# Gate and value products by Strassen's seven products over pairs of 512-token groups, in two runs, with the converted weights kept in scratch memory

## The chip, the cores and the metric

The kernel runs on one core of a Trainium2 chip. The metric is the device time of one execution in microseconds (us). The engines are TensorE (PE in the rows: matmuls; PEld: its weight loads, which run beside the matmuls), VectorE (DVE), ScalarE (ACT), GpSimd (POOL), and SyncE (SP), which issues nearly all transfers.

## The reference: what is computed

An attention-like stage without a softmax makes `x`, 2304 tokens by 512 features. Two layers follow:

```python
h = x @ w_in                                   # 512 -> 2048
g = np.where(h > 0.0, h, np.exp(np.minimum(h, 0.0)) - 1.0)
x = g @ w_out                                  # 2048 -> 512
gate = 1.0 / (1.0 + np.exp(-(x @ w_gate)))     # 512 -> 1536
val = x @ w_val                                # 512 -> 1536
out = gate * val @ w_out2                      # 1536 -> 512
```

The weights come in as 64-bit floats; the kernel makes 32-bit ones of them on the chip. The change is in the second layer, the last four lines.

## The kernel before

**Numbers in two parts.** Each 32-bit operand is split into a high part (the value in TensorE's fp32r format) and a low part (the value minus that). `split` (L79) makes both: ScalarE writes the high part (L81), GpSimd or VectorE the low part (L82). `mm3` (L84) makes one product of three matmuls: high by high, high by low, low by high (L86, L87, L88).

**Tokens and features.** The 2304 tokens are four groups of 512 and one of 256. A layer's hidden features are taken in blocks `f` of 128: 16 in the first layer, 12 in the second. A pass takes two blocks and goes over all groups; the partial outputs of a pass are collected in PSUM tiles `acc` and then added to `y` in SBUF.

**Second layer.** For each block and group, `FF.ups` (L297) makes the gate product into a bank `h` and the value product into a bank `tv`: four blocks of input features by three matmuls each, so 24 matmuls. ScalarE takes the sigmoid of `h` (L314), VectorE multiplies by `tv` (L317), and the result is split into a tile `g` (L81, L82). Two steps later `FF.downs` (L335) uses `g`: for each 128 tokens of the group one `mm3` against `w_out2`, 12 matmuls. In the second block of a pass `evac_b` (L365) copies the sums to `y` (L372) or adds them (L374), and in the last pass stores the rows (L377).

**Weights.** Each block of each weight matrix is loaded once as 512 KB of 64-bit words into one of two buffers `raw` (L111), and converted by `Weight.chain` (L113): two ScalarE instructions (L120, L121), four on VectorE (L123, L124, L127, L129), and a split. The steps of the chain are put between the instructions of the matmul steps. A raw buffer is free again after L129.

**What sets the order.** Everything is written out by hand. Each engine takes its instructions in the order of the program, so an instruction that waits holds up all that stand behind it on its engine. The transfers stand in SyncE's queue in the same way.

## Time and profile before

| | |
|---|---|
| median of 3 runs | 930.99 us (930.36 to 931.33) |
| span of the profiled execution, first to last instruction | 929.7 us |
| PE busy | 911.1 us, 98% |
| DVE, ACT, POOL busy | 469.3, 365.7 and 298.2 us |
| granted TensorE clock, mean | 0.998 |

The span is that of one execution that was profiled; the median of the runs is 1.3 us over it, for what lies before the first and behind the last instruction and from run to run. A busy share is an average over the span. In the rows below a time in us at the start of a row counts from the start of the span, and a matmul's duration includes its way through the array, which overlaps the next one: what one costs in a stream is the distance between two starts.

### The profile page before, as it was taken

To read this page: it belongs to the slowest core of one execution; us is meant where nothing else is said; L and a number is where in the kernel's file an instruction comes from. 1 tells how busy PE (TensorE), PEld (TensorE's weight loads), DVE (VectorE), ACT (ScalarE), POOL (GpSimd) and SP (SyncE) were. 2 spreads that over 40 slices of the span, in tenths; PEclk is the share of its full clock that TensorE was granted. 3 is DMA by queue.
4 is the path that set the end of the run, shared out by engine and by line. 5 is a ranking of instruction groups with operands and counts; after the bars stand their busy time and mean duration, and the time that the engine had idled before them with its cause. 6 is when DMAs were issued, how large, how long until landed. Compare 5 with 4: busy or idle time off the path is not lost.

```text
span 929.7 us, 15480 instructions
## 1 busy us (share of the span) xinstructions
PE 911.1 (98%) x6466; PEld 770.7 (83%) x6466; DVE 469.3 (50%) x759; ACT 365.7 (39%) x675; POOL 298.2 (32%) x259
## 2 busy tenths in 40 slices
PE   7899999999999999999999999999999999999998
PEld 5789988888888888888888888888888888888886
DVE  3767635555464555566884334444435354343223
ACT  2345565544545444545673333323223232221110
POOL 2245523332333333334563213222222233222111
PEclk9999999999999999999999999999999999999999
DMA  9655411210111111102121101111111012000113
GB/s 341 199 181 183 118 46 47 68 35 34 46 47 46 45 46 46 46 25 67 46 68 46 46 23 53 39 46 46 45 46 46 24 46 67 24 23 1 46 46 114
DMA packets 26999, 60.57 MB, mean 65 GB/s; under 512 B 6576, under 2 KB 7600, under 8 KB 26928
## 3 DMA queue, kind: packets, MB, share of 16 engines
q1 hardware_dynamic: 24864, 56.89, 19.0%
q10 hardware_dynamic: 2064, 2.67, 0.8%
q8 instruction: 51, 0.84, 0.4%
q14 instruction: 20, 0.16, 0.1%
HBM read 54.84 MB, written 4.72 MB: 64 GB/s over the span
## 4 chain that ended last, share of the span: by engine, by line
PE 93%; DVE 4%; ACT 1%; DMA 1%; POOL 0%; issue 0%; ACTq 0%; DVEq 0%; POOLq 0%
PE acc L86 12%; PE acc L87 12%; PE acc L88 12%; PE h L86 12%; PE h L88 12%; PE h L87 12%; PE tv L87 5%; PE tv L86 5%; PE tv L88 5%; PE to L194 3%; PE h L290 2%; DMA vt<-in_csmall 1%; PE ts L194 1%; DVE e L266 1%; DVE t L127 0%; DVE t L124 0%
## 5 line engine op out<-in xcount | busy, mean ns | idle before, releaser
L82 POOL TENSOR_TENSOR g<-e,g 128x512 fp32r<-128x512 f32 (+1 forms) x146 | 165.8, 1135 | 565.9 <-ACT g L81 526.3
L86 PE MATMUL h<-x,w 128*128 128x512 f32 (+1 forms) x520 | 192.5, 370 | 0.0
L88 PE MATMUL h<-x,w 128*128 128x512 f32 (+1 forms) x520 | 192.3, 370 | 0.0
L87 PE MATMUL h<-x,w 128*128 128x512 f32 (+1 forms) x520 | 192.3, 370 | 0.0
L81 ACT CAST g<-e 128x512 fp32r<-128x512 f32 (+1 forms) x148 | 82.5, 558 | 232.3 <-DVE e L317 154.7
L317 DVE TENSOR_TENSOR e<-e,tv 128x512 f32<-128x512 f32 (+1 forms) x60 | 38.1, 634 | 231.8 <-PE tv L88 231.8
L86 PE MATMUL acc<-g,w 128*128 128x512 f32 (+1 forms) x352 | 124.3, 353 | 1.2 <-ACT w L81 0.6
L88 PE MATMUL acc<-g,w 128*128 128x512 f32 (+1 forms) x352 | 124.0, 352 | 0.3 <-DVE w L82 0.2
L87 PE MATMUL acc<-g,w 128*128 128x512 f32 (+1 forms) x352 | 123.8, 352 | 0.0
L309 DVE SCALAR_TENSOR_TENSOR e<-e,h 128x512 f32<-128x512 f32 (+1 forms) x88 | 51.9, 590 | 134.8 <-ACT e L306 134.2
L87 PEld LDWEIGHTS h<-x,w 128*128 128x128 f32 x520 | 97.9, 188 | 17.7
L88 PEld LDWEIGHTS h<-x,w 128*128 128x128 f32 x520 | 98.0, 188 | 17.6
L86 PEld LDWEIGHTS h<-x,w 128*128 128x128 f32 x520 | 97.9, 188 | 17.6
L314 ACT ACTIVATE e<-h 128x512 f32<-128x512 f32 (+1 forms) x60 | 33.3, 555 | 154.5 <-PE h L88 150.7
L82 POOL TENSOR_TENSOR w<-t,w 128x512 fp32r<-128x512 f32 x65 | 86.6, 1332 | 8.9 <-ACT w L81 8.7
L305 ACT ACTIVATE e<-h 128x512 f32<-128x512 f32 (+1 forms) x88 | 45.8, 520 | 109.6 <-PE h L88 92.2
L87 PE MATMUL tv<-x,w 128*128 128x512 f32 (+1 forms) x240 | 88.7, 370 | 0.0
L86 PE MATMUL tv<-x,w 128*128 128x512 f32 (+1 forms) x240 | 88.6, 369 | 0.0
L88 PE MATMUL tv<-x,w 128*128 128x512 f32 (+1 forms) x240 | 88.6, 369 | 0.0
L87 PE MATMUL acc<-w,g 128*128 128x512 f32 x216 | 84.6, 392 | 0.0
L86 PE MATMUL acc<-w,g 128*128 128x512 f32 x216 | 84.6, 392 | 0.0
L88 PE MATMUL acc<-w,g 128*128 128x512 f32 x216 | 84.4, 391 | 0.0
(75 smaller groups left out, 1344.5 us busy)
## 6 DMA issues: line engine op xcount, KB each, us to landing
in<-in_ain SPq DMA_DIRECT2D x12, 1024.0 KB, 5.5
raw<-in_w_in SPq DMA_DIRECT2D x16, 512.0 KB, 3.5
raw<-in_w_out SPq DMA_DIRECT2D x14, 512.0 KB, 3.6
raw<-in_w_gate SPq DMA_DIRECT2D x12, 512.0 KB, 3.6
raw<-in_w_val SPq DMA_DIRECT2D x12, 512.0 KB, 3.5
raw<-in_w_o SPq DMA_DIRECT2D x12, 512.0 KB, 3.5
y<-in_ain SPq DMA_DIRECT2D x4, 1024.0 KB, 7.8
out<-y SPq DMA_DIRECT2D x8, 256.0 KB, 2.8
```

The lines of the kernel that those rows point to most:

```text
L81: act.copy(hi, src)
L82: lo_engine.tensor_tensor(out=lo, in0=src, in1=hi.bitcast(F32), op=ALU.subtract)
L86: pe.matmul(out_, wh, xh, start=start, stop=False, skip_group_check=shared)
L87: pe.matmul(out_, wh, xl, start=False, stop=False, skip_group_check=shared)
L88: pe.matmul(out_, wl, xh, start=False, stop=stop, skip_group_check=shared)
L194: return pe.matmul(out_, w, x, start=start, stop=True, skip_group_check=True)
L266: dve.tensor_tensor(out=self.xf.rearrange("d (p x i) -> d x p i", p=NP, x=2), in0=to[:, :, 256:].rearrange("d x (p i) -> d x p i", p=NP), ...
L290: pe.matmul(h, w[:, a, c[k]], x[:, b, k, t], start=i + k == 0, stop=i == 2 and k == KB - 1)
L305: act.activation(out=e, in_=h, func=AF.Relu, scale=-1.0)
L309: dve.scalar_tensor_tensor(out=e, in0=e, scalar=-1.0, in1=h, op0=ALU.add, op1=ALU.max)
L314: act.activation(out=e, in_=h, func=AF.Sigmoid)
L317: dve.tensor_tensor(out=e, in0=e, in1=v, op=ALU.mult)
```

## The change

**Seven products for eight.** Two groups of 512 tokens are a pair. The 512 input features are two halves, so the gate and value products of a pair and a block are a 2 by 2 by 2 product of blocks: eight block products, each of two feature blocks by three matmuls, 48 matmuls. Strassen's scheme (in Winograd's form) makes them of seven, 42 matmuls, from sums of the operands:

- four sums of the tokens' blocks (`Pair.sum`, names t1 to t4), once for each pair;
- four sums of the weights' blocks (`Sums.chain`, tile `s` with both its parts), once for each `f`;
- sums of the products. Three PSUM banks A, B and D are used in a `unit`; products 1, 6, 5 and 3 are accumulated in turn into A, which is copied to SBUF in between, and 7 and 4 into D.

The 256-token group keeps the plain products (`single`).

**Two runs.** The first run takes pair 0 (groups 0 and 1) and the last group through the twelve blocks, the second run takes pair 1 (groups 2 and 3). The weights are converted in the first run as before, and the converted tiles (`w` of gate, half of `w` of value, `s`, `w` of out2: 2.25 MB for each block) are stored to scratch memory (`save`). In the second run they are loaded again (`restore`). The operands of the pairs lie where the first layer's `x` was.

**Order.** The products against `w_out2` (`down`: 128 tokens, two blocks, six matmuls) are kept in a list and put between the products of the units two blocks later (`fill`). The steps of the weight chains of the next block are put between the products as well (`bg`). The split of a unit's results is issued in the next unit (`later`). The low part of the last group's results goes to a part of `x3`. The tiles `e`, `g`, `t` and `w` are taken from rings of named buffers; `e` has six.

```diff
-            t = tpool.tile([128, DM], I32, tag="t", name="t")
+            t = t_tile(self.at)
             f, u = t.bitcast(F32), t.bitcast(U32)
+            self.f = f
...
-            p = wpools[0] if self.i < 8 or (self.i - 8) % 12 >= 4 else wpools[1]
-            w = p.tile([128, 2, DM], F32R, tag="w", name="w")
+            w = w_tile(self.slot)
             split(w[:, 0, :], w[:, 1, :], f, lo_engine)
             self.w = w
...
+    class Sums:
+        def __init__(self, f):
+            self.f = f
+        def chain(self):
+            (g0, g1), (v0, v1) = ((t[:, : DM // 2], t[:, DM // 2 :]) for t in (W[n, self.f].f for n in "gv"))
+            dve.tensor_tensor(out=v1, in0=v0, in1=v1, op=ALU.add)
+            dve.tensor_tensor(out=v0, in0=g0, in1=v0, op=ALU.subtract)
+            yield
+            dve.tensor_tensor(out=g0, in0=v1, in1=g0, op=ALU.subtract)
+            dve.tensor_tensor(out=g1, in0=g1, in1=g0, op=ALU.subtract)
+            yield
+            w = s_tile(self.f)
+            split(w[:, 0, 0], w[:, 1, 0], W["v", self.f].f, pool)
+            split(w[:, 0, 1], w[:, 1, 1], W["g", self.f].f, pool)
+            self.w = w
+            yield
+    for f in range(FB):
+        W["g", f] = Weight(w_gate[f], f % 2 * 3, 0)
+        W["v", f] = Weight(w_val[f], f % 2 * 3 + 1, 1)
+        W["2", f] = Weight(w_o2[f], (2, 6, 5, 7)[f % 4], 2)
+        W["s", f] = Sums(f)
...
+        def sum(self, name):
+            a, b = {"t1": ("12", "11"), "t2": ("22", "t1"), "t3": ("22", "12"), "t4": ("21", "t2")}[name]
+            dve.tensor_tensor(out=self.f32(name), in0=self.f32(a), in1=self.f32(b), op=ALU.subtract)
+        def split(self, name, lo_engine):
+            p = self.place(name)
+            split(p[:, 0], p[:, 1], self.f32(name), lo_engine)
+            self.x[name] = p.rearrange("p i (k t) -> p i k t", k=KH)
+    UP = {1: ("11", "11"), 2: ("12", "21"), 3: ("s4", "22"), 4: ("22", "t4"), 5: ("s1", "t1"), 6: ("s2", "t2"), 7: ("s3", "t3")}
+    def product(i, pair, f, bank, start=False):
+        a, b = UP[i]
+        x = pair.x[b]
+        for k in range(KH):
+            if a[0] == "s":
+                t, at = {"s3": (0, 0), "s1": (0, 2), "s2": (1, 0), "s4": (1, 2)}[a]
+                w = W["s", f].w[:, :, t, (at + k) * 128 : (at + k) * 128 + 128]
+            else:
+                at = ((int(a[1]) - 1) * KH + k) * 128
+                w = W["gv"[int(a[0]) - 1], f].w[:, :, at : at + 128]
+            mm3(bank, w[:, 0], w[:, 1], x[:, 0, k], x[:, 1, k], start and k == 0, k == KH - 1, True)
...
+    def finish_later():
+        while later:
+            later.pop(0)()
+    def unit(pair, f, bg, fill):
+        A, B, D = u_bank(), u_bank(), u_bank()
+        s1, s2, s4, sg = (e_tile() for _ in range(4))
+        product(1, pair, f, A, True)
+        act.copy(s1, A)
+        finish_later()
+        fill(5)
+        bg()
+        product(2, pair, f, B, True)
+        dve.tensor_tensor(out=s1, in0=s1, in1=B, op=ALU.add)
+        bg()
+        fill(0)
+        product(7, pair, f, D, True)
+        bg()
+        product(6, pair, f, A)
+        act.copy(s2, A)
+        act.activation(out=s1, in_=s1, func=AF.Sigmoid)
+        bg()
+        fill(1)
+        product(5, pair, f, A)
+        act.copy(s4, A)
+        dve.tensor_tensor(out=s4, in0=s4, in1=D, op=ALU.add)
+        bg()
+        fill(2)
+        product(3, pair, f, A)
+        act.activation(out=sg, in_=A, func=AF.Sigmoid)
+        fill(3)
+        product(4, pair, f, D)
+        later.append(glu(pair.g + 1, f, sg, s4))
+        dve.tensor_tensor(out=s2, in0=s2, in1=D, op=ALU.add)
+        fill(4)
+        later.append(glu(pair.g, f, s1, s2))
+    def glu(g, f, a, b, engine=pool):
+        engine.tensor_tensor(out=a, in0=a, in1=b, op=ALU.mult)
+        def rest():
+            n = N[g]
+            if g == 4:
+                gt = x_of[3].rearrange("p i k t -> p (i k t)")[:, 2048 + f % 3 * 2 * n : 2048 + (f % 3 + 1) * 2 * n]
+                gt = gt.rearrange("p (i t) -> p i t", i=2)
+            else:
+                gt = g_tile()
+            gb[g, f] = gt
+            split(gt[:, 0], gt[:, 1], a, pool)
+        return rest
...
+    def down(fs, g, t, by):
+        a = acc_bank()
+        c = slice(t * 128, t * 128 + 128)
+        for f in fs:
+            x, w = gb[g, f], W["2", f].w
...
+        prep = {
+            a + 5: (("split", "11", dve), ("split", "21", pool)),
+            a + 7: (("sum", "t1"), ("sum", "t3"), ("split", "t1", dve), ("sum", "t2")),
+            a + 8: (("split", "t2", pool), ("split", "t3", dve)),
+            a + 9: (("split", "22", pool), ("sum", "t4")),
+        }
...
+        def background(f):
+            order = "gvgvgvgvgv2s2s2s22" if 0 < f < FB - 1 else "22222" if f else "2s2s2s22"
+            chains = {n: W[n, f + (n != "2")].chain() for n in set(order)}
+            seen = {n: 0 for n in chains}
+            for n in order:
+                next(chains[n])
+                seen[n] += 1
+                if n != "s" and seen[n] == 4:
+                    at = raws_of.index((n, f + (n != "2"))) + 2
+                    if at < len(raws_of):
+                        W[raws_of[at]].load()
+                if seen[n] == order.count(n):
+                    done.append((n, f + (n != "2")))
+                elif done and n == "2":
+                    save(*done.pop(0))
+                yield
+            while done:
+                save(*done.pop(0))
+        def save(n, f):
+            w = W[n, f].w
+            w = w[:, :, 256:] if n == "v" else w
+            copies[n, f] = dpool.tile(list(w.shape), F32, tag=f"{n}{f}", name=f"{n}{f}")
+            sp.dma_start(out=copies[n, f], in_=w.bitcast(F32))
+        def restore(f, names):
+            for n in names:
+                if n == "s":
+                    W[n, f].w = s_tile(f)
+                    w = W[n, f].w
+                else:
+                    w = W[n, f].w = w_tile(W[n, f].slot)
+                    w = w[:, :, 256:] if n == "v" else w
+                sp.dma_start(out=w.bitcast(F32), in_=copies[n, f])
...
+        hooks = {
+            (0, 0, 5): [lambda: ff[end - 2].downs(nothing), lambda: prepare(pairs[0], (("split", "t4", dve),))],
+            (0, 0, 1): [lambda: ff[end - 1].downs(nothing)],
+            (0, 0, 2): [x_last],
+            (0, FB - 1, 0): [lambda: prepare(pairs[1], (("split", "11", dve),))],
+            (0, FB - 1, 1): [lambda: prepare(pairs[1], (("split", "21", pool),))],
+            (0, FB - 1, 2): [lambda: prepare(pairs[1], (("sum", "t1"), ("sum", "t3")))],
+            (0, FB - 1, 3): [lambda: prepare(pairs[1], (("split", "t1", dve),))],
+            (0, FB - 1, 4): [lambda: prepare(pairs[1], (("sum", "t2"),))],
+            (0, FB - 1, 6): [lambda: prepare(pairs[1], (("split", "t2", pool), ("split", "t3", dve)))],
+            (1, 0, 5): [lambda: prepare(pairs[1], (("split", "22", pool), ("sum", "t4")))],
+            (1, 0, 0): [lambda: prepare(pairs[1], (("split", "t4", dve),))],
...
+        for which, pair in enumerate(pairs):
+            for f in range(FB):
+                new = []
+                if not which:
+                    if f == FB - 1:
+                        restore(0, "gvs")
+                    work = background(f)
+                    bg = stepper(work, 7 + (0, 0, 5)[min(f, 2)], 8 if f == 0 else 5 if f == FB - 1 else 18)
+                else:
+                    restore(f, "2")
+                    if f + 1 < FB:
+                        restore(f + 1, "gvs")
+                    bg = nothing
+                ours = todo[: (len(todo) + 1) // 2] if f % 2 == 0 else todo
+                todo = todo[len(ours) :]
+                at = (1, 2, 3, 4, 2)
+                places = [[d for i, d in enumerate(ours) if at[i] == j] for j in range(7)]
+                def fill(j):
+                    for d in places[j]:
+                        d()
+                        bg()
+                    for h in hooks.get((which, f, j), ()):
+                        h()
+                unit(pair, f, bg, fill)
+                if not which:
+                    single(4, f, bg)
+                    fill(6)
+                    for _ in work:
+                        pass
+                if f % 2:
+                    fs = [f - 1, f]
+                    order = [pair.g + 1, pair.g] + ([] if which else [4])
+                    todo = [lambda fs=fs, g=g, t=t, by=pair.out_by: down(fs, g, t, by) for g in order for t in range(GS[g])]
+        finish_later()
+        for d in todo:
+            d()
```

On **ScalarE**, in the second layer before: two steps of two groups. The names are those of the sections above; the number is the tile's own.

```order
L121 ACTIVATE raw_5706<-raw_5706 128x512
L81 CAST w_5774<-t_5725 128x512 [waits DVE_49]
L314 ACTIVATE e_5777<-h_5778 128x512 [waits PE_49]
L81 CAST g_5808<-e_5777 128x512 [waits DVE_49]
L372 COPY y4_5820<-acc_5763 128x512 [waits PE_49]
L81 CAST w_5823<-t_5771 128x512 [waits DVE_49]
L314 ACTIVATE e_5826<-h_5827 128x512 [waits PE_49,Pool_49]
L81 CAST g_5854<-e_5826 128x512 [waits DVE_49]
L120 ACTIVATE t_5873<-raw_5811 128x512 [waits DMAHW1_49,Pool_49]
L121 ACTIVATE raw_5811<-raw_5811 128x512
L314 ACTIVATE e_5876<-h_5877 128x512 [waits PE_49]
L81 CAST g_5907<-e_5876 128x512 [waits DVE_49]
```

In the changed kernel the same engine from the first product of a unit of the first run to the weights behind its fifth product. `e_5829`, `e_5830` and `e_5831` are copies of bank A after products 1, 6 and 5:

```order
L447 COPY e_5829<-h_5826 128x512 [waits PE_49,Pool_49]
L107 CAST g_5840<-e_5642 128x512 [waits Pool_49]
L107 CAST g_5843<-e_5639 128x512 [waits Pool_49]
L107 CAST x3_113<-e_5782 128x256 [waits DVE_49]
L145 ACTIVATE t_5848<-raw_5711 128x512 [waits DMAHW0_49,Pool_49]
L146 ACTIVATE raw_5711<-raw_5711 128x512
L145 ACTIVATE t_5858<-raw_5816 128x512 [waits DMAHW3_49]
L146 ACTIVATE raw_5816<-raw_5816 128x512
L458 COPY e_5830<-h_5826 128x512 [waits PE_49,Pool_49]
L459 ACTIVATE e_5829<-e_5829 128x512 [waits DVE_49]
L463 COPY e_5831<-h_5826 128x512 [waits PE_49]
L107 CAST w_5903<-t_5848 128x512 [waits DMAHW2_49,DVE_49]
```

Before, each bank `h` was read once, by the sigmoid. Now bank A is read between products, and the reading instructions stand behind splits of the unit before and behind the first two instructions of two weight chains.

On **GpSimd** before, in the same stretch:

```order
L82 TENSOR_TENSOR g_6286<-e_6255,g_6286 128x512 [waits Activation_49]
L82 TENSOR_TENSOR w_6301<-t_6252,w_6301 128x512 [waits Activation_49]
L82 TENSOR_TENSOR g_6335<-e_6304,g_6335 128x512 [waits Activation_49,Pool_49]
L82 TENSOR_TENSOR w_6349<-t_6298,w_6349 128x512 [waits Activation_49]
L82 TENSOR_TENSOR g_6380<-e_6352,g_6380 128x512 [waits Activation_49]
L82 TENSOR_TENSOR g_6433<-e_6402,g_6433 128x512 [waits Activation_49,Pool_49]
L82 TENSOR_TENSOR w_6455<-t_6399,w_6455 128x512 [waits Activation_49]
L82 TENSOR_TENSOR g_6486<-e_6458,g_6486 128x512 [waits Activation_49]
```

In the changed kernel, from the weights of one unit to the splits that follow it:

```order
L108 TENSOR_TENSOR w_5903<-t_5848,w_5903 128x512 [waits DMAHW2_49,PE_49,Activation_49]
L108 TENSOR_TENSOR w_5914<-t_5858,w_5914 128x512 [waits DMAHW3_49,PE_49,Activation_49]
L477 TENSOR_TENSOR e_5832<-e_5832,e_5831 128x512 [waits Activation_49]
L477 TENSOR_TENSOR e_5829<-e_5829,e_5830 128x512 [waits DVE_49]
L108 TENSOR_TENSOR s_5985<-t_5858,s_5985 128x512 [waits DMAHW5_49,Activation_49]
L108 TENSOR_TENSOR s_5985<-t_5848,s_5985 128x512 [waits Activation_49]
L108 TENSOR_TENSOR w_6009<-t_5925,w_6009 128x512 [waits DMAHW0_49,Activation_49]
L108 TENSOR_TENSOR g_6029<-e_5832,g_6029 128x512 [waits Activation_49]
L108 TENSOR_TENSOR g_6032<-e_5829,g_6032 128x512 [waits Activation_49]
L108 TENSOR_TENSOR x3_113<-e_5971,x3_113 128x256 [waits Activation_49]
```

Before, there were low parts alone, one for each result and one for each weight tile. Now the products of gate and value (L477) and two low parts of the weight sums `s` stand among them.

## Rows read from the trace of the kernel before

**Rows 1.** Page: engines' busy time; the chain that ended last, by engine.

```profile
PE 911.1 (98%) x6466; PEld 770.7 (83%) x6466; DVE 469.3 (50%) x759; ACT 365.7 (39%) x675; POOL 298.2 (32%) x259
...
PE 93%; DVE 4%; ACT 1%; DMA 1%; POOL 0%; issue 0%; ACTq 0%; DVEq 0%; POOLq 0%
```

**Rows 2.** Busy time by window: stretch, length, engines' us (instructions), PEclk, DMA share, GB/s.

```profile
430.00:478.00 48.00, 48.00 (x228) 40.03 (x227) 38.18 (x55) 31.57 (x56) 28.54 (x22) 1.00 0.21 64
478.00:700.00 222.00, 222.00 (x1048) 184.91 (x1047) 100.58 (x156) 75.42 (x134) 65.10 (x53) 1.00 0.14 44
700.00:925.00 225.00, 225.00 (x1055) 187.82 (x1053) 86.55 (x134) 53.35 (x94) 51.31 (x42) 1.00 0.13 43
```

**Rows 3.** Timeline, second layer: start, duration, engine, line, tiles [idle before].

```profile
475.11 0.39 PE L86 MATMUL h<-x,w 128*128 128x512 f32 x1
...
913.95 0.28 PE L88 MATMUL tv<-x,w 128*128 128x256 f32 x1
914.07 0.40 PE L86 MATMUL acc<-w,g 128*128 128x512 f32 x1
...
914.34 0.42 DVE L317 TENSOR_TENSOR e<-e,tv 128x256 f32<-128x256 f32 x1 [2.26 <-PE tv L88]
...
924.93 0.39 PE L88 MATMUL acc<-w,g 128*128 128x512 f32 x1
```

**Rows 4.** Timeline behind the last matmul.

```profile
924.67 1.37 DVE L374 TENSOR_TENSOR y<-y,acc 128x512 f32<-128x512 f32 x2 [1.35 <-PE acc L88]
...
925.39 1.18 SPq L377 DMA_DIRECT2D out<-y  x2
```

**Rows 5.** Groups by line and shape, 478 to 925 us: busy, mean ns | idle before.

```profile
L81 ACT CAST g<-e 128x512 fp32r<-128x512 f32 x48 | 29.8, 621 | 136.5 <-DVE e L317 136.5
L314 ACT ACTIVATE e<-h 128x512 f32<-128x512 f32 x48 | 28.7, 598 | 129.4 <-PE h L88 125.6 <-POOL w L82 3.8
L120 ACT ACTIVATE t<-raw 128x512 f32<-128x512 f32 x30 | 19.9, 663 | 0.0
...
L82 POOL TENSOR_TENSOR g<-e,g 128x512 fp32r<-128x512 f32 x48 | 62.2, 1296 | 275.1 <-ACT g L81 275.1
L82 POOL TENSOR_TENSOR w<-t,w 128x512 fp32r<-128x512 f32 x30 | 40.5, 1350 | 6.4 <-ACT w L81 6.4
...
L374 DVE TENSOR_TENSOR y<-y,acc 128x512 f32<-128x512 f32 x89 | 58.5, 685 | 2.4 <-PE acc L88 2.4
L129 DVE SCALAR_TENSOR_TENSOR t<-raw,t 128x512 uint32<-128x512 uint32 x30 | 20.5, 684 | 0.0
L124 DVE TENSOR_SCALAR t<-t 128x512 uint32<-128x512 uint32 x30 | 12.8, 427 | 1.0
```

**Rows 6.** Timeline of VectorE, then of GpSimd, in the same stretch.

```profile
482.18 0.42 DVE L123 TENSOR_SCALAR t<-t 128x512 f32<-128x512 f32 x1
...
483.18 0.69 DVE L127 CUSTOM_DVE_ANT_0 t<-raw,t 128x1024 uint16<-128x1024 uint16 x1
...
485.74 1.05 DVE L123 TENSOR_SCALAR t<-t 128x512 f32<-128x512 f32 x1 [0.67 <-ACT t L120]
...
487.37 1.58 DVE L127 CUSTOM_DVE_ANT_0 t<-raw,t 128x1024 uint16<-128x1024 uint16 x1
...
485.21 1.30 POOL L82 TENSOR_TENSOR g<-e,g 128x512 fp32r<-128x512 f32 x1 [3.49 <-ACT g L81]
486.85 1.55 POOL L82 TENSOR_TENSOR w<-t,w 128x512 fp32r<-128x512 f32 x1 [0.35 <-ACT w L81]
```

**Rows 7.** Timeline of VectorE near the end of the first layer.

```profile
469.68 3.23 DVE L82 TENSOR_TENSOR x<-y,x 128x512 fp32r<-128x512 f32 x2
```

**Rows 8.** Transfers: count, KB each, median us from issue to landing; last one from 50 to 70 us.

```profile
in<-in_ain SPq DMA_DIRECT2D x12, 1024.0 KB, 5.5
...
raw<-in_w_val SPq DMA_DIRECT2D x12, 512.0 KB, 3.5
...
raw<-in_w_in SPq DMA_DIRECT2D x1, 512.0 KB, 7.9
```

More of the change, by code (lines that the diff above doesn't have):

```diff
@@ L327, in sums @@
                 else:
-                    n = KB if self.kind == "a" else self.n // 128
-                    wide = self.n if self.kind == "a" else DM
-                    acc[key] = [psum["acc"].tile([128, 512], F32, tag="acc", name="acc")[:, :wide] for _ in range(n)]
+                    acc[key] = [acc_bank()[:, : self.n] for _ in range(KB)]
             return acc[key]
@@ new lines, in retention_elu_glu @@
+        gb = {}
+        copies = {}
+        raws_of = [("2", 0)]
+        for f in range(1, FB):
+            raws_of += [("g", f + 1), ("v", f + 1), ("2", f)] if f + 1 < FB else [("2", f)]
+        done = []
+        def background(f):
[16 more added lines that the diff above has]
+                save(*done.pop(0))
```

216 lines of the change are left out of this document (134 added, 82 removed).

## The prediction

> **What bounds the kernel now.** I read the page first, then busy time by window, then TensorE's timeline over the second layer. The busy list and the chain of waits [rows 1] show TensorE busy in 98% of the span and holding 93% of the chain. The windows [rows 2] show the second layer, 475 to 925 us, without a gap: PE busy 222.00 of 222.00 and 225.00 of 225.00 us at a granted clock of 1.00 (2.4 GHz), with VectorE at 45 and 38%, GpSimd at 29 and 23% and transfers at 44 GB/s. So the stage is priced in matmuls. It runs from 475.11 to 924.93 us [rows 3]; a 256-wide matmul starts 0.12 us after the one before it (913.95 to 914.07). The stage holds 1800 matmuls of 512 columns and 312 of 256 (24 of them left from the first layer): (450.05 - 312 x 0.12) / 1800 = 0.2292 us for each of 512. That, not the 0.39 us of a row, is what one costs.
>
> **The change, part by part.**
>
> *Removed.* 48 matmuls become 42 for each pair and block: 6 x 2 pairs x 12 blocks = 144 fewer, and nothing is added on TensorE. 144 x 0.2292 = 33.0 us. All of it lies on the path, since nothing else bounded the stage. A block now takes (42 + 30) x 0.2292 + 24 x 0.12 = 19.4 us of matmuls in the first run and (42 + 24) x 0.2292 = 15.1 in the second. The rest of the sum is what the new waits give back.
>
> *Entry into the stage.* The first pair's sums and splits join the first layer's last pass. On VectorE, between the first sum (t1) and the last reading of bank D that product 4 of the first unit needs, stand seven new instructions of 1024 elements (four sums, the low parts of t1, t3, t4). With them stand eight adds to y of 512 and four of 256, three results of the first layer, a weight chain and the first half of another, four half-wide weight sums and two adds of products: at the durations of [rows 5, 6] about 15 us, against 25 us of matmuls in the same stretch. The price of a 1024-wide one is not in the trace: two 512-wide L129 give 1.4 us (uncontended), the two splits of [rows 7] 3.2 us (beside GpSimd's splits). The sum is then 25 to 37 us. I take 1.8, nearer to the L129 row, since GpSimd is busy about two thirds of this stretch and not throughout: 27.6 us. Walking TensorE through it, it waits 2.6 us for banks of y that are not yet added, and 0.9 us for the last group's operands. 3.5 us, bounds 0 to 12.
>
> *The second unit* has no out2 products to put between its own. Product 5 overwrites nothing, but adds to bank A only after the copy of product 6's state, and product 3 after the next copy. From a matmul's end to the reader is 0.11 us (914.23 to 914.34 [rows 3]), the reading takes 0.60 (L314 [rows 5]), some 0.1 back: 0.8 us, twice, 1.6. Bounds 0 (were the copies early) and 4.2, if ScalarE first takes two conversions of 0.66 each time.
>
> *The first run's ten other units.* Here six matmuls (1.38 us) of out2 stand between products 6 and 5, and cover the 0.8 us if ScalarE and its output buffer are free. ScalarE has 20 instructions, about 12.5 us of 19.4. The copy of product 6 goes to a buffer of the ring of six that GpSimd still reads as the former unit's results (its wait names GpSimd in the order). GpSimd's chain, from the start of a unit's product 1: VectorE's add to y of the last out2 product (16.6 to 17.2), two weight sums (18.0), ScalarE's high part of s (18.7), then five low parts on GpSimd (two of s, one of w, two of g), 3 x 1.35 + 2 x 1.30 = 6.65 us [rows 5]: 25.4, which is 6.0 of the next unit. The copy then ends at 6.7 and product 5 is due at 6.9. The margin is 0.2 us, and a low part that meets VectorE takes 1.55 instead of 1.30 [rows 6]; with two or three such I take 0.4 us lost in each unit, 4.0 in all. Bounds 0 and 14 (the second rival). Cover: were the out2 product not there, each unit would lose 0.8 us twice.
>
> *SyncE's queue.* Each block of the first run adds four stores (0.5, 0.25, 1 and 0.5 MB) between the raw loads. A load waits behind a store's own wait; in the order a store's low part is done before the load's raw buffer is free, so I take nothing here (upper bound: the third rival).
>
> *Between the runs* the second pair's t3 must be split before product 7: two high parts of 1024 on ScalarE, then a low part on VectorE, from about 19.0 of the last unit to 22.5, against 22.2 needed and possibly 1 us more. 0.7 us, bounds 0 to 3. *In the second run* VectorE has some 7 instructions in 15.1 us and GpSimd 4; the loads are 2.25 MB in 15.1 us, by 5.5 us for 1 MB and 3.5 for 0.5 [rows 8] some 8 to 13 us if one after the other. Nothing lost, upper bound 2 us.
>
> *The end.* GpSimd's last product and low part are ready 3.3 us after product 4, TensorE has 1.38 + 0.7 + 0.46 us of other work: 0.9 waits. Now one tile, not two, is added behind the last matmul ([rows 4]: 1.37 for two), minus 0.6. 0.3 us.
>
> Sum: -33.0 + 3.5 + 1.6 + 4.0 + 0.7 + 0.3 = -22.9. The profiled execution's span is 929.7, so 906.8; the median lies 1.3 above its span, so **908.1 us**.
>
> **A rule to weigh.** [rows 6] show L123 at 0.42 us alone and at 1.05 when it started inside a GpSimd instruction (485.21 to 486.51), ending 0.28 us behind it; L127 takes 0.69 alone and 1.58 beside another, ending 0.55 behind it. The Trainium skill (SBUF — State Buffer, section "Who interferes with whom") says that GpSimd and VectorE share a port pair as an exclusive lock, which instructions of VectorE with two SBUF inputs or in a two-port mode need: the later one waits for the whole of the other. The two pairs of rows agree with that. If it holds for every such instruction it makes the second rival.
>
> **The rivals.**
>
> 1. *Everything is hidden.* VectorE keeps up at the entry and the 0.2 us of margin hold: only the second unit and the end remain, -33.0 + 1.6 + 0.3 = -31.1: 899.9 us. For it: VectorE at 45% before. Against it: [rows 7], and GpSimd's work per block, which grows from 4.5 x 1.30 + 3 x 1.35 = 9.9 us in some 37 to 12.6 in 19.4.
>
> 2. *GpSimd and VectorE exclude each other, and the first run is paced by both together.* GpSimd per block: 5 x 1.35 for weights, 4.5 x 1.30 for results and their products: 12.6 us. VectorE's instructions that use no PSUM: 3 x (0.42 + 0.43 + 0.69 + 0.68) for three chains and four half-wide sums (1.4): 8.1. One after the other 20.7 us, 1.3 over the 19.4 of matmuls, 14 us over eleven blocks in place of the 4.0: 918.1 us. For it: [rows 6]. Against: L129 and L124 keep their 0.68 and 0.43 us in the mean [rows 5], so not all exclude.
>
> 3. *The raw loads pace the first run, and it is slower.* Two raw buffers serve three loads per block, so there is a loop: value load, conversion, release, out2 load, conversion, release. With loads of 3.5 us, 0.66 on ScalarE, and VectorE's chain between (5.1 and 5.5 us with the adds that stand ahead), the loop is 18.9 us against 19.4. Each us that a load takes longer adds two to the loop. Traffic grows from 44 to 3.75 MB / 19.4 us = 193 GB/s, and a load that was issued behind a 1 MB one took 7.9 us [rows 8]. At 5.5 us for each load the loop is 22.9 us, ten blocks lose 35: 904.1 + 35 = 939 us. From 5.1 us on the kernel is not faster. Against: in SyncE's order the 1 MB store stands behind the value load, and has some 5 us before the out2 load.
>
> **How the numbers follow.** Forecast 0.57, all hidden 0.15, port 0.18, loads 0.08; 0.02 for a mixture of the last two that ends at no change. The forecast's own range is 900 to 915. With the first two rivals inside and the bounds of the entry, 897 to 925; the lower end is the removed work with nothing given back, 898, less 1 for the runs' spread. Faster by over 0.2% (about what a measurement of this kernel can tell from no change, 1.9 us): 0.57 + 0.15 + 0.18 = 0.90; within it 0.02; slower 0.08.
>
> **What would show it.** Right: 144 fewer matmuls at the same 0.23 us; PE gaps in the first two units of the stage of some 5 us in all; units of the first run at 19.4 to 20.2 us, with gaps before product 5, released by ScalarE's copy, and that one by GpSimd; units of the second run at 15.1 without gaps; raw loads at 3.5 us. Rival 2: gaps spread over products 6, 5 and 4, L148 and L152 (L123 and L127 of before) at 1 and 1.6 us throughout. Rival 3: ScalarE waiting at L145 for a load. The forecast is wrong if units of the first run take over 20.7 us, if the second run has gaps, or if the granted clock falls after the waits at the entry.

## The result, and the profile after

The changed kernel takes 936.72 us (median of 6 runs, 932.85 to 938.95); the kernel before took 930.84 beside it. The ratio is 1.006, 95% interval 1.0043 to 1.0077: slower, where 908.0 us was forecast. The profiled execution, the slowest of the six, took 938.95 us with a span of 937.2, against 929.7 before.

The page's busy list and the chain of waits by engine, answering to [rows 1]:

```profile
PE 894.9 (95%) x6322; PEld 750.1 (80%) x6322; DVE 546.5 (58%) x838; ACT 418.2 (45%) x766; POOL 408.9 (44%) x327
...
PE 67%; DVE 14%; issue 6%; POOL 6%; ACT 5%; DMA 2%; ACTq 0%; POOLq 0%; DVEq 0%; SPq 0%
```

The 144 matmuls are gone (6466 to 6322), but TensorE's share of the chain fell from 93 to 67%: other engines now set the time for a third of the span. Busy time by window shows where, as in [rows 2] (columns as there): the entry, the second unit, one steady unit of the first run, and 160 us of the second run.

```profile
478.00:500.00 22.00, 19.06 (x98) 16.50 (x99) 12.64 (x24) 11.95 (x21) 11.89 (x9) 0.92 0.45 166
500.00:520.00 20.00, 15.95 (x68) 12.79 (x67) 14.10 (x20) 9.20 (x18) 11.57 (x10) 0.83 0.45 171
589.40:610.50 21.10, 19.79 (x96) 16.32 (x96) 17.58 (x26) 10.87 (x20) 13.38 (x11) 1.00 0.53 186
740.00:900.00 160.00, 160.00 (x695) 130.13 (x694) 49.59 (x71) 43.34 (x77) 55.40 (x43) 1.00 0.47 173
```

The second run has no gap. A unit of the first run takes 21.1 us instead of 19.4. TensorE's timeline gives the gaps, in brackets the idle time and who ended it:

```profile
503.86 0.50 PE L112 MATMUL u<-x,s 128*128 128x512 f32 x1 [1.18 <-ACT e L458]
...
508.40 0.80 PE L112 MATMUL u<-x,s 128*128 128x512 f32 x1 [2.87 <-ACT e L463]
508.99 0.63 PE L113 MATMUL u<-x,s 128*128 128x512 f32 x1
509.42 0.63 PE L114 MATMUL u<-x,s 128*128 128x512 f32 x1
...
611.19 0.50 PE L112 MATMUL h<-x,s 128*128 128x512 f32 x1 [1.39 <-ACT e L458]
...
736.72 0.80 PE L113 MATMUL h<-x,s 128*128 128x512 f32 x1 [2.09 <-DVE x L108]
...
932.46 0.39 PE L112 MATMUL acc<-w,g 128*128 128x512 f32 x1
932.68 0.39 PE L113 MATMUL acc<-w,g 128*128 128x512 f32 x1
932.91 0.39 PE L114 MATMUL acc<-w,g 128*128 128x512 f32 x1
```

The gaps at 503.86 and 611.19 stand before product 5, which waits for ScalarE's copy of product 6's state (L458); a wait like the one at 611.19 comes in nine of the ten other units (1.2 to 2.1 us). From 508.99 to 509.42 a matmul takes 0.43 us instead of 0.23: behind a wait of 2.87 us the granted clock was at its lower level (1.2 GHz) for a while. Before, every window of this layer read 1.00 [rows 2]; this one reads 0.83.

The account, from the start of each TensorE instruction and its distance to the one before beyond 0.229 us (0.12 for 256 columns): entry 5.1, second unit 7.2 (2.9 of it the lower clock), ten other units 16.7 (1.4 of it the clock), between the runs 5.2 (1.3 of it the clock), before the last matmuls 1.0. With 5.3 in distances under 0.15 us each from 490 us on and about 1.1 of lower clock at the entry that is 41.6. The changed kernel came to the entry 0.6 us earlier (the matmul that starts at 422.37 us before starts at 421.79), so 41.6 - 33.0 - 0.6 = 8.0, and the last matmul moved from 924.93 [rows 3] to 932.91.

What the copy waits for is seen one step back. ScalarE's timeline, then VectorE's and GpSimd's, in one unit:

```profile
597.05 0.67 ACT L145 ACTIVATE t<-raw 128x512 f32<-128x512 f32 x1 [1.84 <-DMA raw<-in_w_o]
...
604.12 0.62 ACT L107 CAST s<-t 128x512 fp32r<-128x512 f32 x1 [4.86 <-DVE t L184]
...
609.20 0.67 ACT L145 ACTIVATE t<-raw 128x512 f32<-128x512 f32 x1 [0.17 <-DMA raw<-in_w_val]
...
610.55 0.59 ACT L458 COPY e<-h 128x512 f32<-128x512 f32 x1
```

```profile
598.39 0.42 DVE L148 TENSOR_SCALAR t<-t 128x512 f32<-128x512 f32 x1
598.85 1.56 DVE L149 TENSOR_SCALAR t<-t 128x512 uint32<-128x512 uint32 x1
...
601.53 1.13 DVE L183 TENSOR_TENSOR t<-t 128x256 f32<-128x256 f32 x1
602.70 1.40 DVE L184 TENSOR_TENSOR t<-t 128x256 f32<-128x256 f32 x1
```

```profile
598.84 1.29 POOL L477 TENSOR_TENSOR e<-e 128x512 f32<-128x512 f32 x1 [1.87 <-ACT e L468]
601.08 1.29 POOL L477 TENSOR_TENSOR e<-e 128x512 f32<-128x512 f32 x1 [0.96 <-DVE e L472]
602.33 1.48 POOL L108 TENSOR_TENSOR s<-t,s 128x512 fp32r<-128x512 f32 x1
```

The copy stands in ScalarE's queue behind a conversion (L145) that waits for a raw load, and the load for a raw buffer that VectorE's conversion frees. It is a loop of ScalarE, VectorE, GpSimd and transfers without a matmul in it. In that loop VectorE's short steps are long where they meet GpSimd: the three long ones above each began inside a GpSimd instruction and ended 0.28 or 0.29 us behind it (600.13 and 600.41 for the first). Of the 32 L149 from 478 to 735 us, the 21 that began inside a GpSimd instruction took 0.83 to 1.56 us and the other 11 took 0.43. VectorE's groups by shape over two units (count | busy, mean ns):

```profile
L149 DVE TENSOR_SCALAR t<-t 128x512 uint32<-128x512 uint32 x7 | 8.1, 1150 | 0.2
L148 DVE TENSOR_SCALAR t<-t 128x512 f32<-128x512 f32 x6 | 4.5, 746 | 2.5 <-ACT t L145 2.5
...
L184 DVE TENSOR_TENSOR t<-t 128x256 f32<-128x256 f32 x2 | 2.8, 1398 | 0.1
L183 DVE TENSOR_TENSOR t<-t 128x256 f32<-128x256 f32 x2 | 2.3, 1136 | 0.0
```

L149 is L124 of before, which had a mean of 0.427 us [rows 5]; here it is 1.15. With 0.42 as the price of each alone, three L149, three L148 and the two sums are stretched by 2.2 + 1.0 + 0.7 + 1.0 = 4.9 us in a unit.

### The profile page after: what moved, and what is told of

The parts are those of the page before. It is cut to its first block, busy times and chain, and to the rows that moved or that the text cites. A ratio compares the mean times of both kernels' runs of the same rounds, so it can differ in the third digit from the quotient of the medians.

```text
span 937.2 us, 15632 instructions
## 1 busy us (share of the span) xinstructions
PE 894.9 (95%) x6322; PEld 750.1 (80%) x6322; DVE 546.5 (58%) x838; ACT 418.2 (45%) x766; POOL 408.9 (44%) x327
## 4 chain that ended last, share of the span: by engine, by line
PE 67%; DVE 14%; issue 6%; POOL 6%; ACT 5%; DMA 2%; ACTq 0%; POOLq 0%; DVEq 0%; SPq 0%
PE acc L112 10%; PE acc L114 10%; PE acc L113 10%; PE h L113 8%; PE h L112 8%; PE h L114 8%; PE to L241 3%; PE u L112 3%; PE u L113 3%; PE u L114 3%; POOL w L108 2%; DVE t L149 2%; PE h L337 2%; DVE t L152 2%; DVE t L154 2%
## 5 line engine op out<-in xcount | busy, mean ns | idle before, releaser
L112 PE MATMUL h<-x,w 128*128 128x512 f32 (+1 forms) x400 | 145.4, 363 | 0.3 <-DVE e L351 0.3
L113 PE MATMUL h<-x,w 128*128 128x512 f32 (+1 forms) x400 | 145.3, 363 | 0.0
L114 PE MATMUL h<-x,w 128*128 128x512 f32 (+1 forms) x400 | 144.8, 362 | 0.0
L477 POOL TENSOR_TENSOR e<-e 128x512 f32<-128x512 f32 x48 | 63.0, 1313 | 142.5 <-ACT e L468 99.9
L107 ACT CAST g<-e 128x512 fp32r<-128x512 f32 (+1 forms) x136 | 75.3, 571 | 81.2 <-DVE e L351 74.7
L518 DVE TENSOR_TENSOR y<-y,acc 128x512 f32<-128x512 f32 x90 | 61.0, 684 | 68.4 <-PE acc L114 68.0
L347 ACT ACTIVATE e<-h 128x512 f32<-128x512 f32 (+1 forms) x88 | 45.9, 521 | 115.7 <-PE h L114 101.9
L112 PEld LDWEIGHTS h<-x,w 128*128 128x128 f32 x400 | 75.8, 189 | 13.0 <-DVE e L351 0.7
L113 PEld LDWEIGHTS h<-x,w 128*128 128x128 f32 x400 | 75.7, 189 | 11.9
L114 PEld LDWEIGHTS h<-x,w 128*128 128x128 f32 x400 | 75.6, 189 | 12.0
L387 DVE TENSOR_TENSOR y<-y,acc 128x512 f32<-128x512 f32 (+1 forms) x140 | 79.2, 628 | 0.1
L112 PEld LDWEIGHTS acc<-g,w 128*128 128x128 f32 x352 | 67.0, 190 | 15.0 <-ACT g L107 4.0
L114 PE MATMUL acc<-w,g 128*128 128x512 f32 x192 | 75.7, 394 | 0.8 <-POOL g L108 0.8
L112 PE MATMUL acc<-w,g 128*128 128x512 f32 x192 | 76.0, 396 | 0.0
L113 PE MATMUL acc<-w,g 128*128 128x512 f32 x192 | 76.0, 396 | 0.0
L114 PEld LDWEIGHTS acc<-g,w 128*128 128x128 f32 x352 | 67.1, 190 | 10.1 <-DVE w L108 0.4
```

The lines of the kernel that those rows point to most:

```text
L107: act.copy(hi, src)
L112: pe.matmul(out_, wh, xh, start=start, stop=False, skip_group_check=shared)
L113: pe.matmul(out_, wh, xl, start=False, stop=False, skip_group_check=shared)
L114: pe.matmul(out_, wl, xh, start=False, stop=stop, skip_group_check=shared)
L347: act.activation(out=e, in_=h, func=AF.Relu, scale=-1.0)
L387: dve.tensor_tensor(out=y[:, e], in0=y[:, e], in1=a, op=ALU.add)
```

## The experiments

Line numbers are those of each kernel, up to 11 off. The "period" is from one unit's L458 copy to the next, in the steady units.

**Third raw buffer.** A third raw buffer in place of one of six `g` buffers; each load goes out one weight earlier.

```
-                g_tile.more(right, 2)
+                g_tile.more(right, 1)
                 t_tile.more(right, 1)
+                r_tile.more(right, 1)
...
-                    at = raws_of.index((n, f + (n != "2"))) + 2
+                    at = raws_of.index((n, f + (n != "2"))) + 3
```

> The changed kernel with a third raw buffer, each load one place earlier in SyncE's order, and five g tiles for six (to make room). Loop theory: the units of the first run are paced, not by TensorE, but by the closed loop of two raw buffers (value load, conversion, release, out2 load, conversion, release), 21.1 us for 19.4 of matmuls; with a third buffer the two loads leave the loop, units take 19.5 to 20.1 us, and the kernel 921 to 927 us. Throughput theory: GpSimd and VectorE exclude each other so often that their work alone takes 21 us; then the loads merely come earlier, units stay at 20.8 to 21.2 and the kernel at 934 to 938 us. Traffic theory (stores slow the loads): loads that stand earlier gain a part, 928 to 933 us.

Measured: 935.05 us, ratio 1.0053 (1.0033 to 1.0072); period 21.1 as before. No conversion waits for a load any more, but the copy starts at the same point. ScalarE's timeline:

```profile
603.39 0.65 ACT L147 ACTIVATE raw<-raw 128x512 int32<-128x512 uint32 x1
604.43 0.59 ACT L459 COPY e<-h 128x512 f32<-128x512 f32 x1 [0.39 <-POOL g L109]
```

Four conversions still stand ahead of it, to 604.04, and then GpSimd reads the buffer it wants. The loads alone are not the cause.

**Fewer stores.** Only block 0's converted weights are stored, and the second run reads block 0's for every block (so its products are not the reference's).

```
         def save(n, f):
+            if f:
+                return
...
-                sp.dma_start(out=w.bitcast(F32), in_=copies[n, f])
+                sp.dma_start(out=w.bitcast(F32), in_=copies[n, 0])
```

> The changed kernel without the stores of blocks 1 to 11; the second run loads block 0's stored weights twelve times, so its results are not the reference's, and its traffic is unchanged. Traffic theory: without 2.25 MB of stores a block the raw loads land sooner, units of the first run fall below 20 us, 920 to 928 us in all. Loop and throughput theories: the two loads that the loop holds land in 3.5 to 3.7 us already, the same as before the change, so units stay at 20.9 to 21.2 us and the kernel at 933 to 938 us.

Measured: 937.23 us (one run), period 21.1. A unit from 589 to 610 us moved 76 GB/s instead of 186. The stores cost nothing that this run shows.

**Product 6's copy first.** The background steps ahead of it in the queues move behind it.

```
-        bg()
         fill(0)
         product(7, pair, f, D, True)
-        bg()
         product(6, pair, f, A)
         act.copy(s2, A)
         act.activation(out=s1, in_=s1, func=AF.Sigmoid)
+        bg()
+        bg()
         bg()
```

> The changed kernel with the weight-chain steps behind products 2 and 7 moved behind product 6's copy and sigmoid, so that on ScalarE the copy which product 5 waits for no longer stands behind the conversion of the value weights. Queue-order theory: the wait before product 5 was due to that place alone; units of the first run take 19.5 to 19.9 us, the kernel 920 to 925 us. Loop theory: product 5's wait goes, but the loop is as long or, with the conversion starting later, up to 1.3 us longer; TensorE waits at another product (7, 6 or the next 1) and units take 21.0 to 22.5 us, the kernel 935 to 952 us.

Measured: 943.38 us (one run), period 22.0: slower. The list of ScalarE's waits, 530 to 720 us (us in total, times, longest), shows why; the changed kernel has 1.8 us in the line for GpSimd.

```profile
ACT t L145 <- DMA raw<-in_w_o: 15.6, 9, 2.0
ACT e L456 <- POOL g L108: 10.8, 8, 1.5
```

First in its queue, the copy waits for GpSimd's low part of `g` instead, and the conversions behind it start later.

**Matmuls in the longest waits.** 28 matmuls whose result nothing reads, in three waits (one of the three here).

```
+    def keep_busy(pair, f, n):
+        a = acc_bank()
+        w, x = W["g", f].w, pair.x["11"]
+        for i in range(n):
+            pe.matmul(a, w[:, 0, :128], x[:, 0, 0], start=i == 0, stop=i == n - 1)
...
+        if (pair.g, f) == (0, 1):
+            keep_busy(pair, f, 11)
         product(3, pair, f, A)
```

> The changed kernel with 28 matmuls whose results nobody reads in the three longest waits: 4 and 11 before products 5 and 3 of the first run's second unit, 13 before product 7 of the second run's first unit. Clock theory: the granted clock fell to half for 6.8 and 3.4 us just behind those waits; with TensorE kept busy it stays at 1.00 there, which gives back 13 and 7 matmuls of 0.42 instead of 0.23 us, 3 to 4.5 us in all: 932 to 934 us. Rival: the extra matmuls lie on the path or the clock does not matter to the end, since the next units wait for the weights anyway (the loop takes it up): 936 to 938 us.

Measured: 934.43 us, 1.004 (1.0025 to 1.0055); mean clock 0.996 instead of 0.987. The window of the second unit, for the clock (0.83 after the change, 0.99 here):

```profile
500.00:520.00 20.00, 17.40 (x85) 13.80 (x84) 15.86 (x20) 9.54 (x19) 12.72 (x11) 0.99 0.42 145
```

That is 2.3 us below the changed kernel, whose own runs spread over 6 us, so the price of the lower clock is uncertain here (the last pair of kernels below shows it better); the units stay at about 21.1.

**Three obstacles at once.** `s1, s4, s2, sg` instead of `s1, s2, s4, sg` gives product 6's copy the buffer that the first gate product freed, not the one GpSimd reads last. This edit went alone, with the copy first, with three raw buffers, and with both.

```
-        s1, s2, s4, sg = (e_tile() for _ in range(4))
+        s1, s4, s2, sg = (e_tile() for _ in range(4))
```

> One edit: the unit takes its SBUF buffers in the order s1, s4, s2, sg instead of s1, s2, s4, sg, so that product 6's copy no longer lands in the buffer whose last reader is GpSimd's low part of the unit before. Theory of three causes in parallel (in each unit of the first run product 5 waits for product 6's copy; the copy waits for (a) ScalarE's queue, in which it stands behind four instructions of the weight conversion, (b) those four for the loads into two raw buffers, and (c) the buffer that GpSimd is still reading): (a) and (b) stay, so the time stays at 934 to 938 us. Rival, the GpSimd buffer alone sets the wait: the wait of about 1.5 us before product 5 goes in the ten units, 918 to 924 us. Rival, VectorE and GpSimd's conversion work is simply the bound of a unit at 21.1 us: 935 to 938 us here and in the three kernels beside it.

> The buffer order of the kernel beside it, and product 6's copy and sigmoid ahead of the weight conversion's steps in ScalarE's queue. Three causes in parallel: the copy runs when product 6 ends, the 1.5 us go before product 5, but the conversion starts about 1.5 us later than before in a loop through two raw buffers (in the earlier kernel with the copy first, whose copy waited 1.5 us for GpSimd, a unit took 22.0 us), so a unit takes 20.4 to 20.9 us: 928 to 934 us. GpSimd buffer alone: 918 to 924 us, as beside it. Conversion work as the bound: 935 to 944 us.

> The buffer order and three raw buffers (loads one weight further ahead), conversion's steps where they were in ScalarE's queue. Three causes in parallel: the copy still stands behind four conversion instructions (2.3 us) in ScalarE's queue, free at about 0.4 us before GpSimd's release, so 0.4 us of 1.5 go in each unit: 929 to 933 us. GpSimd buffer alone: 918 to 924 us. Conversion work as the bound: 933 to 937 us.

> All three: buffer order, three raw buffers, product 6's copy and sigmoid first. Three causes in parallel: nothing is left of the wait before product 5, a unit of the first run takes 19.4 to 19.9 us instead of 21.1, nine or ten such units: 917 to 924 us, faster than the kernel before. GpSimd buffer alone: the same 917 to 924 us, but then the kernel with the buffer order alone has it too. Conversion work as the bound: 933 to 944 us, with VectorE or GpSimd busy without a pause through a unit.

Measured: 935.69 (1.006), 934.1 (1.0036), 933.4 (1.0025) and 932.69 us (1.0023, 1.0013 to 1.0033). My theory of three causes in parallel failed on the last: all three obstacles are gone, no steady unit waits before product 5, and the period is still 21.16 us. TensorE now waits before product 7. TensorE's row, then two of ScalarE's:

```profile
622.33 0.50 PE L113 MATMUL u<-x,s 128*128 128x512 f32 x1 [1.16 <-ACT e L504]
```

```profile
621.37 0.62 ACT L108 CAST s<-t 128x512 fp32r<-128x512 f32 x1 [4.46 <-DVE t L185]
621.89 0.38 ACT L504 ACTIVATE e<-u 128x256 f32<-128x256 f32 x1
```

The sigmoid that frees the bank stands behind the high part of `s`, and that behind VectorE's last sum (L185). The third theory is left, though the second and fourth kernel came out 0.9 and 0.3 us under its ranges: the conversion itself is the period.

**Sums on GpSimd**, alone, with the three edits, and with two places more (first diff, all four sums); **low parts on VectorE**, with the three edits (second diff, every low part of weights and sums).

```
-            dve.tensor_tensor(out=v1, in0=v0, in1=v1, op=ALU.add)
+            pool.tensor_tensor(out=v1, in0=v0, in1=v1, op=ALU.add)
...
```

```
-            split(w[:, 0, 0], w[:, 1, 0], W["v", self.f].f, pool)
+            split(w[:, 0, 0], w[:, 1, 0], W["v", self.f].f, dve)
...
```

> One edit to the changed kernel: the four sums of each weight pair (128x256, in place) run on GpSimd instead of VectorE, where they took 1.13 to 1.51 us beside a busy GpSimd and 0.42 us alone. Theory, a serial conversion chain of 21.1 us per unit (ScalarE, VectorE, GpSimd one after the other for one weight block, VectorE's steps stretched beside GpSimd) is the period of the first run: VectorE loses 4.5 us of the chain, GpSimd gains about 3.2 us (four of some 0.8 us, estimated from 0.90 us for its 128x256 low part), but the two raw buffers and the buffer that GpSimd reads stay, so a unit takes 19.6 to 20.6 us and the time is 924 to 931 us. Rival, the amount of conversion work (VectorE and GpSimd together) sets the unit wherever it stands: 20.9 to 21.4 us a unit, 933 to 938 us. Rival, GpSimd is the bound and gets worse: over 21.5 us a unit, above 939 us.

> Sums on GpSimd, and with them the three edits of the kernel before this one (buffer order, product 6's copy first, three raw buffers), which by themselves left the unit at 21.15 us with the wait moved from product 5 to product 7, for GpSimd's low parts of the sums. Serial chain: nothing is left on the chain that is longer than the matmuls' 19.4 us but about 0.4 us: units of 19.4 to 20.1 us, 917 to 924 us, faster than the kernel before. Amount of work: 20.9 us or more a unit, 931 to 936 us. GpSimd as the bound: above 936 us.

> As the kernel beside it, and two places more: in the second unit two conversion steps stand behind product 5's copy instead of ahead of it (the wait of 3.5 us before product 3 and the half clock behind it, 2.5 us), and the second pair's t2 and t3 are split two steps earlier, as soon as the products that read their places are done (waits of 1.4 and 2.3 us between the runs and the half clock behind them, 1.3 us). Serial chain: 3 to 7 us below the kernel beside it, 911 to 919 us. If the second unit's wait is only put off into the third: 0 to 3 us below it. Amount of work: 926 to 933 us.

> The three edits, with the sums on VectorE as in the changed kernel, and the low parts of weights and sums on VectorE instead of GpSimd (0.69 us each there by the 128x512 sums of two SBUF inputs, against 1.3 to 1.75 us). Serial chain: low parts of a block shorten by about 0.6 to 1.1 us, three of the four sums no longer meet a busy GpSimd (2 us), 2 us of low parts are added to VectorE: 19.8 to 20.5 us a unit, 919 to 927 us. Amount of work: VectorE then has about 18 us of its own, 20.9 us or more a unit, 931 us or above. If contention with GpSimd is not what stretches VectorE's steps, L150 and the sums stay at 1.1 to 1.5 us though GpSimd has less than half its work.

Measured: 933.55 (1.0023), 926.32 (0.9952, 0.9934 to 0.9971), 927.01 (0.9957) and 924.41 us (three runs; 0.9935, 0.9914 to 0.9956). The periods are 20.8, 20.4, 20.4 and 20.5: both directions shorten the chain, the first three by less than I expected (the first and the third lie in the ranges of the amount of work). The two places of the third gave nothing: the wait of 3.45 us in the second unit came back as one of 3.92 us in the third. In the last, GpSimd has 6.3 us of work left in a unit and still stretches what it meets (L149 to 1.50 us, L150 to 0.85, L182 to 1.40, L184 to 1.15). That left two readings, stretch beside GpSimd or amount of work.

**GpSimd emptied.** Its last work in the units, the gate products and the low parts of their results, goes to VectorE too, beside the low parts of weights and sums (second diff above): with the three edits, and then in the changed kernel with nothing else edited.

```
-    def glu(g, f, a, b, engine=pool):
+    def glu(g, f, a, b, engine=dve):
...
-            split(gt[:, 0], gt[:, 1], a, pool)
+            split(gt[:, 0], gt[:, 1], a, dve)
```

> The kernel with the low parts on VectorE, and the last of GpSimd's work in the units too: the two gate products and the low parts of their results (GpSimd 6.3 us a unit) go to VectorE, where their 128x512 instructions take about 0.62 us each from start to start (some 3.1 us a unit). Theory, VectorE's steps are stretched by GpSimd's work beside them: VectorE's short steps (0.42 us alone) no longer meet GpSimd, which gives back about 3.2 us a unit (in the kernel before this one they took 1.50, 0.85, 1.40 and 1.15 us), so VectorE's 18.9 us stay about 18.8 and the unit at 19.6 to 20.7 us: 918 to 928 us. Rival, the stretch has another cause and the amount of work is the bound: VectorE needs 22 us or more, a unit 22 to 23.7 us, 940 to 960 us.

> The changed kernel with one thing edited: low parts of weights, sums and gate products, and the gate products themselves, run on VectorE instead of GpSimd; buffers, buffer order and the queue's order as in the changed kernel. Theory, VectorE's stretch beside GpSimd is the cause, and the other three only decide where the wait shows: the conversion chain through two raw buffers takes its uncontended 18.9 us or a little more, a unit 19.5 to 20.4 us, 917 to 928 us. Rival, all four are needed: the loads into two raw buffers still end the chain, 20.9 us a unit or more, 932 to 940 us.

Measured with the three edits: 918.26 us, 0.9862 (0.9842 to 0.9881), period 19.9, without a wait of TensorE in the steady units. A window of 19.5 us of a unit (GpSimd is the fifth engine), then VectorE's groups over two such windows:

```profile
598.00:617.50 19.50, 19.50 (x96) 16.17 (x96) 18.15 (x35) 10.31 (x20) 0.00 (x0) 1.00 0.58 196
```

```profile
L150 DVE TENSOR_SCALAR t<-t 128x512 uint32<-128x512 uint32 x6 | 2.6, 428 | 0.2
L149 DVE TENSOR_SCALAR t<-t 128x512 f32<-128x512 f32 x5 | 2.1, 423 | 1.0 <-ACT t L146 1.0
...
L185 DVE TENSOR_TENSOR t<-t 128x256 f32<-128x256 f32 x2 | 0.8, 425 | 0.1
L184 DVE TENSOR_TENSOR t<-t 128x256 f32<-128x256 f32 x2 | 0.8, 420 | 0.0
```

VectorE does 35 instructions in the window, where it did 26 in 21.1 us, and needs 18.15 us instead of 17.58 (18.55 over the whole 19.9); each short step is back at 0.42 us. The amount of work is not the bound. What the low parts of weights and sums gave includes that they are shorter on VectorE (0.69 us against 1.3 to 1.75). The last move is free of that, since the gate products and the low parts of `g` are no steps of the conversion: VectorE takes five instructions more in a unit (31 to 36), is busy 18.55 us instead of 18.9, and the kernel gains another 6 us. What this move takes away in VectorE's row is the stretch of the four steps named above, 3.2 us in a unit. With nothing else edited, GpSimd emptied gives 929.53 us (0.9985, 0.9973 to 0.9996), periods 20.5 to 21.2: copy and conversion wait for the loads again, in ScalarE's timeline:

```profile
603.07 0.68 ACT L145 ACTIVATE t<-raw 128x512 f32<-128x512 f32 x1 [0.64 <-DMA raw<-in_w_val]
```

That lies between the two expectations: GpSimd emptied alone is worth 7.2 us, the three edits alone 4.0, both together 18.5. Of the single steps tried, emptying GpSimd gives the most, and it is not the whole; how much of its 7.2 us is the stretch and how much the shorter low parts was not separated.

**A balance.** The three edits, sums on GpSimd, the sums' low parts on VectorE behind the w2 conversion's last VectorE step; then the same with the 28 matmuls.

```
-            order = "gvgvgvgvgv2s2s2s22" if 0 < f < FB - 1 else "22222" if f else "2s2s2s22"
+            order = "gvgvgvgvgv2s2s22s2" if 0 < f < FB - 1 else "22222" if f else "2s2s2s22"
```

> Buffer order, copy first, three raw buffers, sums on GpSimd (20.4 us a unit so far, GpSimd 16.75 us busy, VectorE 16.0), and now the sums' low parts on VectorE, behind the last step of the w2 conversion: GpSimd 14.2 us, VectorE about 17.4. GpSimd's low parts of g come 2.5 us sooner, and the next conversion no longer waits 0.5 us for GpSimd's reading of the sums. Serial chain: 19.4 to 20.0 us a unit, 914 to 922 us. Rival, what GpSimd gives up VectorE loses again (the chain passes through both): 20.3 to 20.9 us a unit, 925 to 931 us.

> The kernel beside it with 28 matmuls of 128 columns, whose result nothing reads, in the waits of the second unit and between the runs. If the half clock behind these waits costs what the rows show (2.5 us and 1.3 us), 2 to 4 us below the kernel beside it; if the matmuls only take the place of the wait and the rest comes later anyway, 0 to 1 us.

(The second text is wrong in one word: the 28 matmuls have 512 columns.) Measured: 917.73 (0.9856, 0.9842 to 0.9871) and 914.77 us (0.9824, 0.9809 to 0.9839). The period is 19.4 to 19.5, the matmuls' own time. Window of the second unit in the one and in the other, for the clock:

```profile
500.00:520.00 20.00, 16.41 (x76) 13.16 (x76) 13.85 (x20) 11.54 (x23) 14.41 (x13) 0.91 0.62 231
```

```profile
500.00:520.00 20.00, 19.61 (x96) 15.86 (x95) 14.96 (x20) 12.36 (x25) 15.20 (x14) 1.00 0.66 244
```

The last one is the fastest version found, 1.8% below the kernel before.

## Why the prediction was wrong

- *Removed work*, 33.0 us: right in the main. 144 fewer matmuls; the second run's later units take 15.15 to 15.32 us (15.1 forecast), without a gap. The matmuls left start a little later than 0.229 us after each other, most of all those with weights from `s` (0.004 to 0.006 us in the second run); that is the 5.3 us of small distances, a term that the sum did not have.
- *The first run's ten other units*, 4.0 us with an upper bound of 14: 16.7. This is the step that failed. The wait was where I put it, before product 5 and for the copy I named, but not for the reason: GpSimd's buffer held the copy in three units from 530 to 720 us, 1.8 us in all. I had made it a condition that ScalarE is free, and checked that by ScalarE's sum, 12.5 of 19.4 us. The copy stands behind four instructions of the conversion, and these come when the conversion's loop lets them, which is every 21.1 us. VectorE's steps in that loop I took from a stretch in which GpSimd was busy 29% of the time [rows 2, 5]; in the first run it is 63% (13.38 of 21.1), and eight of its short steps in a unit take 0.75 to 1.4 us in the mean instead of 0.42, 4.9 us together. Emptying GpSimd gave 7.2 us by itself and 14.4 on top of the three edits.
- *Rival 2* had the mechanism, and its 14 us for these units was near the 16.7; it came out at 918.1 us because it kept the forecast's other terms and put the clock at nothing. Its reckoning, the two engines' work added up to 20.7 us, was near in part by luck: what sets the period is a serial chain through ScalarE, VectorE, GpSimd and the loads, in which they also wait for one another (VectorE was busy 17.58 of 21.1 us). In the balanced kernel the same reckoning gives about 21 us (estimated from the same durations, with 0.74 to 0.80 for a sum on GpSimd) and the period is 19.5. And I held the unstretched means of L129 and L124 against it [rows 5]. They say nothing on it: of the 30 L124 and 30 L129 from 478 to 925 us none began inside a GpSimd instruction. In the changed kernel the step of L127 (L152) took 1.78 us the one time that it did, and in the balanced kernel the step that L129 has become (L155) takes 1.11. GpSimd's row, then VectorE's:

```profile
609.13 1.27 POOL L184 TENSOR_TENSOR t<-t 128x256 f32<-128x256 f32 x1
```

```profile
609.84 1.11 DVE L155 SCALAR_TENSOR_TENSOR t<-raw,t 128x512 uint32<-128x512 uint32 x1
```

  The Trainium skill (SBUF — State Buffer, section "Who interferes with whom") has the port pair of the two engines as an exclusive lock; that short steps fall back to 0.42 us in the kernel with an empty GpSimd agrees.
- *Rival 3*: its loop was there (conversions wait for loads, 1.84 us at 597.05), but the two loads in it took 3.5 and 3.7 us and not 5.5, and its 18.9 us became 21.1 by VectorE's steps. A third raw buffer alone gave 1.7 us, inside the spread of the runs.
- *The second unit*, 1.6 (0 to 4.2): 7.2. Both copies were late as forecast, but the second stood behind two casts that waited 2.30 us for VectorE, and the clock fell behind the wait.
- *Entry*, 3.5 (0 to 12): 5.1. *Between the runs*, 0.7 (0 to 3): 5.2, as the low part of t3 came late on VectorE. *End*, 0.3: 0.5 (1.0 of waits, and 0.5 less behind the last matmul). *Stores*, nothing: right.
- *The clock* I named as what would make the forecast wrong, and gave no price: by the rows of the profiled execution 1.1 at the entry, 2.9 in the second unit, 1.4 in one of the ten and 1.3 between the runs, 6.7 in all. It differs between runs of one kernel (mean granted clock 0.987 to 0.995 in the six). 2.3 us (inside the spread of the runs) and 3.0 came back in the two pairs of kernels that differ by the 28 matmuls.

What stays open: how the 7.2 us of the emptied GpSimd divide, why the second unit's wait moves to the third when its casts are put off, and how much of the entry could be had; none was tried further.

## What to carry to other kernels

When matmuls are taken from a stage that TensorE fills, the next period can be a loop, as here, and not an engine's sum: follow one block's conversion through every engine and back to its own buffer, and price VectorE's steps as they are beside a GpSimd as busy as it will be then. Where removing an obstacle moves the wait and not the time, several paths may have nearly the same length, and only removing them together shows it. Work taken from GpSimd and given to a VectorE that is already the busier can shorten the stage: with the three edits VectorE's busy time in a unit rose from 17.64 to 18.55 us, and the kernel gained 14.4. A mean near the alone price shows only that an instruction has not met GpSimd yet.

## What the hardware showed that I had not expected

- VectorE's 128x512 step on one SBUF tensor takes 0.42 us alone and 0.75 to 1.15 us in the mean beside a GpSimd that is 63% busy; its adds of a PSUM bank to SBUF kept 0.68 us in the same unit.
- In a kernel whose TensorE is 95% busy the granted clock fell to its lower level (1.2 GHz) with four of the five waits of 2.1 to 2.9 us, and not with the fifth (2.12 us before 717.51). It is not the same each time: with the wait of 2.42 us at the entry the window from 478 to 490 us reads 0.86 in the changed and in the last kernel and 1.00 in the balanced one. Matmuls put into two of the five waits and into a shorter one kept the clock at 0.99 to 1.00 there; the last kernel is 3.0 us faster than the balanced one by them.
